# Eight single PSUM banks, sums of g by DMA and a new hand-written order in an attention and MLP kernel

## The chip, the cores and the metric

The kernel runs on one core of one Trainium2 chip. The metric is the time of the kernel on the device, in microseconds (us); of several runs the median is given. The engines that matter are TensorE (PE, matmuls), VectorE (DVE), ScalarE (ACT) and GpSimd (POOL); SP issues transfers. PE writes its results to PSUM, which has eight banks of 512 float32 columns on each of 128 partitions. DVE and ACT read them from there.

## What is computed

There are four batches of 6080 tokens with 256 channels, and q, k, v of that shape. The attention runs over channels: a 256 x 256 matrix for each batch. A token-wise MLP with 2048 hidden features follows.

```python
qn = q / (np.linalg.norm(q, axis=1, keepdims=True) + 1e-06)
kn = k / (np.linalg.norm(k, axis=1, keepdims=True) + 1e-06)
s = kn.transpose(0, 2, 1) @ qn / tau
a = softmax(s)                       # over the last axis
x = (v @ a).reshape(B * N, 256)
h = x @ w_in                         # 256 -> 2048
g = 0.5 * h * (1.0 + np.tanh(c * (h + 0.044715 * h * h * h)))
out = g @ w_out                      # 2048 -> 256
```

## The kernel before, in words

The product a @ w_in is made once for each batch ("aw", 256 x 2048 in bf16), so that the main part has two stages: h = v @ aw, then out = gelu(h) @ w_out. The tokens are cut into 25 blocks: each batch has five of 1024 tokens and one of 960, the last batch ends with 512 and 448. A block has two halves of 512 (480) tokens, and 16 chunks of 128 hidden features.

**First stage.** Chunks come in two ways. A *plain* chunk (word `g`, `plain`, L495) is two halves of two matmuls with 512 columns each. They fill a pair of PSUM banks, and one gelu over 1024 elements reads both (`G`, L511). In block 0 `e` and `E` (L522, L534) do the same for two chunks of one half. A *set* (words `m1` to `m7`, `small`, L563) makes two chunks, i and 8 + i, of both halves with seven matmuls in place of eight, by a scheme of the Strassen kind on sums of aw (`SW`) and of v (`vs`). Its additions go over ACT and DVE (`set_step`, L607): `wcq` copies bank rb into the first bank of a pair qp (ACT), `wy5` copies the second bank to SBUF (ACT), `wap` and `wax` add rb and that copy (DVE), and PE adds further products onto what they left in PSUM. `wGq` is the gelu over both banks of the pair, `wGr` and `wGx` are the gelus of the other two quarters. Over all blocks 137 pairs of chunks are sets and 110 chunks are plain.

**Second stage.** It is a scheme of the same kind with products M1 to M7 (`product`, L712), each of four matmuls for each half h of the features, on sums of g, T1 to T4 (`token_sum`, L693). They are adds of 128 x 2048 bf16 elements on DVE. In the blocks that `SUMS_DMA` (L952) names, T3 is a transfer instead: POOL issues a DMA that adds one quarter of g onto another in SBUF. M7 reads T3. `cq`, `y5`, `ap` and `ax` are the stage's additions (`mm2_step`, L765), `c11` to `c22` transpose the results on DVE (`turn`, L744), and SP stores them.

**Beside it.** For each later batch q and k are loaded in eight pieces by POOL (`lq`, `lk`). They are squared (`qsq`, `ksq`: on ACT, or on DVE where `SQ_DVE`, L949, says so), folded (`f1` to `f3`), summed on PE (`sp`) and multiplied on PE (`row`), and a chain of small steps makes that batch's aw (`aw`, `ac`). POOL casts v to bf16 in HBM (`lv`), and SP loads it transposed (`lt`).

**Order.** There is no scheduler. `ORDER` (L958) is a list of 3498 words; each word records its instructions on its engines, and every engine works through its own in that order. A word `m1.5@r:2` is product m1 of set 5 in block 2, and it takes the PSUM buffer with the tag r. There are two pairs (h, b) and four single banks (a, p, r, s). A tag is taken again only when the last reader of its earlier contents is done. POOL's loads wait for the matmul just before them in the list (`GATE`), so that they don't run ahead.

Of the kernel before, what the change touches and what calls it, by code (L numbers as in the profile page):

```python
# [16 lines left out]
def kernel(  # L17
# [228 lines left out]
    def ss_rows(c, which, rows=None):  # L246
# [3 lines left out]
        if c == 0:  # L250
            SS[which] = bank("sp"[which], [128, 2] if which == 0 else [128, 256], f"ss0{which}")
# [135 lines left out]
    def first_aw():  # L387
        b = 0
        ps0 = [bank("sp"[ic], [128, 256], f"aw_ps{ic}") for ic in range(2)]
        ps1 = bank("b", [128, 2, 512], "aw_ps")  # L390
        ps = [ps0, [ps1[:, ic, 0:256] for ic in range(2)]]
        sums = bank("a", [128, 2], "sums0")
# [92 lines left out]
    PAIR_USES = {}  # L485

    def apart(n, i, side, engine, inst):

        uses = PAIR_USES.setdefault((n, i), [])
        for other, s, e in uses:  # L490
            if s != side and e != engine:
                tc.declare_no_dep(inst.ins, other.ins.name, reason="the other bank of the pair")
        uses.append((inst, side, engine))

    def plain(n, u, tag):  # L495
# [6 lines left out]
        w = hc if wide else t
        for x in range(2):
            BITS[tag, x] = w
            for cc in range(2):
                mm(hp[:, x, :w],
                   lhsT=aw(b, cc, u if wide else 2 * u + x),
                   rhs=vt_tiles[n][:, cc, x * hc : x * hc + hc] if wide else vt_tiles[n][:, cc, :],
                   start=cc == 0, stop=cc == 1)

    def plain_gelu(n, u):  # L511
        t = BLOCKS[n][2]
        hc = t // 2
        hp = PR.pop((n, u))
        if t > 512:
            nc.scalar.activation(g_half(n, u // 8)[:, :, u % 8], hp[:, :, :hc], AF.Gelu_apprx_tanh)  # L516
        else:
            k0 = u % 4 * 2
            nc.scalar.activation(g_half(n, u // 4)[:, :, k0 : k0 + 2].rearrange("p t u x -> p u t x"),
                                 hp[:, :, :t].rearrange("p u (t x) -> p u t x", t=2), AF.Gelu_apprx_tanh)  # L520

    def half(n, p, t, tag):  # L522

        b = batch(n)
        hc = hc_of(n)
        hp = bank(tag, [128, 2, 512], f"e{n}_{p}_{t}")
        PR[n, p, t] = hp
        for x in range(2):
            BITS[tag, x] = hc
            for cc in range(2):  # L530
                mm(hp[:, x, :hc], lhsT=aw(b, cc, 2 * p + x),
                   rhs=vt_tiles[n][:, cc, t * hc : t * hc + hc], start=cc == 0, stop=cc == 1)
# [30 lines left out]
    def small(n, i, m, tag=None):  # L563
# [16 lines left out]
        if m == 1:  # L580
            RB[n, i] = bank(tag, [128, 512], f"rb{n}_{i}")
        if m == 5:
            QP[n, i] = bank(tag, [128, 2, 512], f"qp{n}_{i}")
            QTAG[n, i] = tag
            w = U * hc
            if BITS.get((tag, 0), 0) < w:
                x0 = BITS.get((tag, 0), 0) // 32 * 32
                for x in range(x0, w, 256):
                    y = min(w, x + 256)
                    mm(QP[n, i][:, 0, x:y], lhsT=ones_bf, rhs=zeros_bf[:, 0 : y - x],  # L590
                       start=x == 0, stop=True)
            BITS[tag, 0] = max(w, BITS.get((tag, 0), 0))
            BITS[tag, 1] = w
        dst = {2: 0, 3: 1, 5: 1}
        acc = QP[n, i][:, dst[m]] if m in dst else RB[n, i]
        for u in range(U):
            inst = mm(acc[:, u * hc : u * hc + hc], lhsT=lhs(u), rhs=rhs,
                      start=m in (1, 5) and u == 0, stop=u == U - 1)
            if m in dst:
                apart(n, i, dst[m], "pe", inst)  # L600
# [6 lines left out]
    def set_step(n, i, what):  # L607
# [4 lines left out]
        if what == "cq":  # L612
            apart(n, i, 0, "act", nc.scalar.activation(QP[n, i][:, 0, :w], RB[n, i][:, :w], AF.Copy))  # L613
# [11 lines left out]
        if what == "Gq":  # L625
            g = g_half(n, 0)
            qp = QP.pop((n, i))
            if U == 1:
# [136 lines left out]
    def mm2_step(n, what):  # L765
        hc = hc_of(n)
        if what == "cq":
            nc.scalar.activation(ACC[n, "p"][:, :hc], ACC[n, "r"][:, :hc], AF.Copy)
        elif what == "y5":
            XS[n] = xp.tile([128, 512], FP32, tag="y5", name=f"y5_{n}")  # L770
            nc.scalar.activation(XS[n][:, :hc], ACC[n, "p"][:, :hc], AF.Copy)
        elif what == "ap":
            nc.vector.tensor_add(ACC[n, "r"][:, :hc], ACC[n, "p"][:, :hc], XS[n][:, :hc])
# [5 lines left out]
        else:  # L779
# [9 lines left out]
    with tc.manual_schedule():
# [88 lines left out]
        def run(word):  # L878
# [42 lines left out]
            elif what == "e":  # L921
                half(n, *a, tag)
            elif what == "E":
                half_gelu(n, *a)
# [366 lines left out]
```

## Time and profile before

| | |
|---|---|
| median of 3 runs | 687.28 us (687.09 to 691.3) |
| the profiled execution | 686.68 us |
| its span, first to last instruction | 684.8 us |
| PE busy, 3584 matmuls | 666.8 us |
| ACT busy, 941 instructions | 620.5 us |
| DVE busy, 924 instructions | 614.0 us |
| POOL busy | 86.5 us |
| granted PE clock, mean | 0.998 |

A group of instructions in the profile is named by its line, engine, output and inputs; all matmuls of the main part have the line of the helper `mm`, L482, so they are told apart by tiles: h, qp and rb belong to the first stage, r and p to the second, G to the q and k products. [...] Busy time counts overlapping instructions once. A share of DMA is the time of all packets over 16 engines' time and can pass 1, as packets overlap.

### The profile page before, as it was taken

To read this page: it belongs to the slowest core of one execution; us is meant where nothing else is said; L and a number is where in the kernel's file an instruction comes from. 1 tells how busy PE (TensorE), PEld (TensorE's weight loads), DVE (VectorE), ACT (ScalarE), POOL (GpSimd) and SP (SyncE) were. 2 spreads that over 40 slices of the span, in tenths; PEclk is the share of its full clock that TensorE was granted. 3 is DMA by queue.
4 is the path that set the end of the run, shared out by engine and by line. 5 is a ranking of instruction groups with operands and counts; after the bars stand their busy time and mean duration, and the time that the engine had idled before them with its cause. 6 is when DMAs were issued, how large, how long until landed. Compare 5 with 4: busy or idle time off the path is not lost.

```text
span 684.8 us, 10307 instructions
## 1 busy us (share of the span) xinstructions
PE 666.8 (97%) x3584; PEld 336.6 (49%) x3584; DVE 614.0 (90%) x924; ACT 620.5 (91%) x941; POOL 86.5 (13%) x151
## 2 busy tenths in 40 slices
PE   3999999999999999999999999999999999999996
PEld 2854545454445454444444544545444444444566
DVE  3579999999999999979999999999999989889894
ACT  4389999998899999989989999999989999999983
POOL 4322111111001101111010010001000011101001
PEclk9999999999999999999999999999999999999999
DMA  9998989694787785875957987657274299378463
GB/s 240 208 247 144 157 152 137 106 153 78 119 119 126 134 156 87 151 114 88 166 87 126 179 136 125 94 85 122 42 113 92 35 138 162 62 119 158 90 118 64
DMA packets 163524, 86.14 MB, mean 126 GB/s; under 512 B 148736, under 2 KB 152448, under 8 KB 162752
## 3 DMA queue, kind: packets, MB, share of 16 engines
q0 software_dynamic: 16496, 47.06, 41.6%
q1 hardware_dynamic: 145728, 37.14, 31.4%
q10 hardware_dynamic: 1248, 1.28, 0.7%
q8 instruction: 28, 0.46, 0.3%
q14 instruction: 24, 0.20, 0.1%
HBM read 78.91 MB, written 36.57 MB: 169 GB/s over the span
## 4 chain that ended last, share of the span: by engine, by line
PE 91%; DMA 4%; ACT 3%; issue 1%; DVE 1%; POOL 0%; DVEq 0%; ACTq 0%; POOLq 0%
PE p L482 23%; PE r L482 18%; PE rb L482 17%; PE qp L482 12%; PE h L482 11%; PE G L205 5%; DMA qk_g1b<-in_k_dram 3%; PE e L482 2%; PE awp L374 2%; DMA qk_g1a<-in_q_dram 1%; PE o L482 1%; ACT g L639 1%; ACT g L629 1%; ACT g L516 0%; ACT qp L613 0%
## 5 line engine op out<-in xcount | busy, mean ns | idle before, releaser
L482 PEld LDWEIGHTS <-wcomb 128*128 128x128 bf16 x1408 | 136.6, 98 | 146.5 <-issue 2.8
L482 PE MATMUL p<-t,wcomb 128*128 128x512 bf16 (+2 forms) x576 | 142.2, 373 | 0.2
L482 PE MATMUL r<-g,wcomb 128*128 128x512 bf16 (+2 forms) x576 | 141.8, 373 | 0.0
L629 ACT ACTIVATE g<-qp 128x1024 bf16<-128x1024 f32 (+1 forms) x130 | 132.1, 1022 | 5.0 <-PE qp L482 4.8
L482 PEld LDWEIGHTS <-aw 128*128 128x128 bf16 x872 | 84.7, 98 | 90.7 <-DVE aw L416 1.3
L708 DVE TENSOR_TENSOR t<-g,t 128x2048 bf16<-128x2048 bf16 (+2 forms) x96 | 112.5, 1180 | 0.0
L621 DVE TENSOR_TENSOR qp<-rb,yw 128x512 f32<-128x512 f32 (+2 forms) x137 | 93.4, 686 | 14.3 <-PE rb L482 6.2
L482 PE MATMUL rb<-tv,sw 128*128 128x512 bf16 (+3 forms) x288 | 100.3, 366 | 0.4 <-ACT qp L613 0.3
L624 DVE TENSOR_TENSOR xw<-rb,yw 128x512 f32<-128x512 f32 (+2 forms) x137 | 92.1, 675 | 6.4 <-PE rb L482 3.9
L516 ACT ACTIVATE g<-h 128x1024 bf16<-128x1024 f32 (+1 forms) x92 | 94.3, 1035 | 2.1 <-PE h L482 2.1
L482 PE MATMUL h<-vT,aw 128*128 128x512 bf16 (+2 forms) x376 | 94.4, 377 | 0.0
L613 ACT ACTIVATE qp<-rb 128x512 f32<-128x512 f32 (+2 forms) x137 | 81.4, 600 | 7.8 <-PE rb L482 6.4
L619 ACT ACTIVATE yw<-qp 128x512 f32<-128x512 f32 (+2 forms) x137 | 81.8, 604 | 6.5 <-PE qp L482 5.0
L482 PEld LDWEIGHTS <-sw 128*128 128x128 bf16 x576 | 56.0, 98 | 56.3 <-issue 2.2
L639 ACT ACTIVATE g<-xw 128x512 bf16<-128x512 f32 (+1 forms) x130 | 82.6, 639 | 0.8 <-DVE xw L624 0.7
L639 ACT ACTIVATE g<-rb 128x512 bf16<-128x512 f32 (+1 forms) x130 | 77.9, 606 | 4.1 <-PE rb L482 3.7
L442 POOL DMA_DIRECT2D vb<-in_v_dram x45 | 22.9, 510 | 305.4 <-PE rb L482 137.9
L708 DVE TENSOR_TENSOR t<-g 128x2048 bf16<-128x2048 bf16 (+2 forms) x48 | 56.3, 1182 | 1.7 <-PE p L482 1.1
L482 PE MATMUL qp<-vT,sw 128*128 128x512 bf16 (+3 forms) x144 | 51.3, 366 | 0.1
L482 PE MATMUL rb<-vT,aw 128*128 128x512 bf16 (+3 forms) x144 | 51.0, 366 | 0.0
L482 PE MATMUL qp<-vT,aw 128*128 128x512 bf16 (+3 forms) x144 | 50.5, 366 | 0.0
L482 PE MATMUL rb<-tv,aw 128*128 128x512 bf16 (+3 forms) x144 | 50.3, 366 | 0.0
(144 smaller groups left out, 816.4 us busy)
## 6 DMA issues: line engine op xcount, KB each, us to landing
out_dram<-ot SPq DMA_DIRECT2D x160, 128.0 KB, 3.1
vb<-in_v_dram POOLq DMA_DIRECT2D x38, 256.0 KB, 3.9
k<-in_k_dram POOLq DMA_DIRECT2D x21, 384.0 KB, 5.9
q<-in_q_dram POOLq DMA_DIRECT2D x21, 384.0 KB, 5.3
g<-g POOLq DMA_DIRECT2D x14, 512.0 KB, 6.1
out_dram<-ot SPq DMA_DIRECT2D x24, 120.0 KB, 3.3
wst<-in_moe_w_out_dram POOLq DMA_DIRECT2D x2, 1024.0 KB, 10.4
vb<-in_v_dram POOLq DMA_DIRECT2D x6, 240.0 KB, 3.8
```

The source lines that it names most:

```text
L205: nc.tensor.matmul(G[b][:, jc, :], lhsT=qt[:np_, r, jc * 128 : jc * 128 + 128], rhs=kt[:np_, r, :], start=first and jc == 0, stop=jc == 1, ...
L374: nc.tensor.matmul(ps, lhsT=ET[b][:, jc, ic * 128 : ic * 128 + 128], rhs=win_bf[:, jc, fs * 512 : fs * 512 + 512], start=jc == 0, stop=jc ...
L442: after(nc.gpsimd.dma_start(out=vb[: y - x, :], in_=v[b, t0 + x : t0 + y, :]), gate)
L482: GATE[0] = nc.tensor.matmul(*a, skip_group_check=True, **kw)
L516: nc.scalar.activation(g_half(n, u // 8)[:, :, u % 8], hp[:, :, :hc], AF.Gelu_apprx_tanh)
L613: apart(n, i, 0, "act", nc.scalar.activation(QP[n, i][:, 0, :w], RB[n, i][:, :w], AF.Copy))
L619: apart(n, i, 1, "act", nc.scalar.activation(YW[n, i][:, :w], QP[n, i][:, 1, :w], AF.Copy))
L621: apart(n, i, 1, "dve", nc.vector.tensor_add(QP[n, i][:, 1, :w], RB[n, i][:, :w], YW[n, i][:, :w]))
L624: nc.vector.tensor_add(XW[n, i][:, :w], RB[n, i][:, :w], YW.pop((n, i))[:, :w])
L629: nc.scalar.activation(g[:, :, k0], qp[:, :, :hc], AF.Gelu_apprx_tanh)
L639: nc.scalar.activation(g[:, t, k0], x[:, :w], AF.Gelu_apprx_tanh)
L708: (nc.vector.tensor_add if add else nc.vector.tensor_sub)(o, a, b)
```

## The change

- PSUM is eight tags of one bank each (a to g, and z, which takes G, `sp`, the small results of a batch and, in the last batch, `m5`). A plain chunk is two words, one for each bank, and each has a gelu of 512 elements. `e` and `E` are gone. In a set m5 has a bank until `wy5` has copied it; the two sums that the pair held are taken when `wcq` and `wap` write them. The gelu `wGq` becomes `wGp` and `wGs`. The second stage's sums are split in the same way (r, m, p, q). `apart`, which declared the two banks of a pair independent, is gone.
- `fill` writes zeros by a matmul where a bank is wider used than a matmul has written it before. In the built order that happens eight times.
- `SUMS_DMA` names blocks 1 to 22 instead of 8, 9 and 18 to 22.
- `SQ_DVE` has 30 squares instead of 12.
- 150 sets instead of 137, so 84 plain chunks (168 half words) instead of 110.
- All 3946 words stand in a new order.

```diff
-    def gram_row(b, c, i, tag="a"):
+    def gram_row(b, c, i, tag="z"):
...
+    def fill(acc, tag, w):
+        x0 = BITS.get(tag, 0) // 32 * 32
+        for x in range(x0, w, 256):
+            mm(acc[:, x : min(w, x + 256)], lhsT=ones_bf, rhs=zeros_bf[:, 0 : min(w, x + 256) - x],
+               start=x == 0, stop=True)
+        BITS[tag] = max(w, BITS.get(tag, 0))
...
-            nc.scalar.activation(g_half(n, u // 8)[:, :, u % 8], hp[:, :, :hc], AF.Gelu_apprx_tanh)
+            nc.scalar.activation(g_half(n, u // 8)[:, x, u % 8], hp[:, :hc], AF.Gelu_apprx_tanh)
...
+    def set_sum(n, i, x, tag):
+        hc = hc_of(n)
+        Q[n, i, x] = bank(tag, [128, 512], f"q{n}_{i}_{x}")
+        fill(Q[n, i, x], tag, hc if hc > 256 else 2 * hc)
...
         if what == "cq":
-            apart(n, i, 0, "act", nc.scalar.activation(QP[n, i][:, 0, :w], RB[n, i][:, :w], AF.Copy))
+            set_sum(n, i, 0, tag)
+            nc.scalar.activation(Q[n, i, 0][:, :w], RB[n, i][:, :w], AF.Copy)
...
         if what == "ap":
-            apart(n, i, 1, "dve", nc.vector.tensor_add(QP[n, i][:, 1, :w], RB[n, i][:, :w], YW[n, i][:, :w]))
+            set_sum(n, i, 1, tag)
+            nc.vector.tensor_add(Q[n, i, 1][:, :w], RB[n, i][:, :w], YW[n, i][:, :w])
...
-        if what == "Gq":
-            g = g_half(n, 0)
-            qp = QP.pop((n, i))
-            if U == 1:
-                nc.scalar.activation(g[:, :, k0], qp[:, :, :hc], AF.Gelu_apprx_tanh)
...
-        acc = "r" if i <= 3 else "p"
+        acc = {1: "r", 2: "r", 3: "q", 4: "p", 5: "m", 6: "p", 7: "p"}[i]
...
-SUMS_DMA = {8, 9, 18, 19, 20, 21, 22}
+SUMS_DMA = {1, 2, 3, 4, 5, 6, 7, 8, 9, 10, 11, 12, 13, 14, 15, 16, 17, 18, 19, 20, 21, 22}
```

More of the change, by code (lines that the diff above doesn't have):

```diff
@@ L250, in ss_rows @@
         if c == 0:
-            SS[which] = bank("sp"[which], [128, 2] if which == 0 else [128, 256], f"ss0{which}")
+            SS[which] = bank("ab"[which], [128, 2] if which == 0 else [128, 256], f"ss0{which}")
         for r in rows:
@@ L266, in warm @@
     def warm(n):
-        w = bank("h", [128, 2, 512], "warm")
+        w = bank("c", [128, 512], "warm")
         for i in range(n):
-            nc.tensor.matmul(w[:, 0, 0:256], lhsT=ones_bf, rhs=zeros_bf, start=True, stop=True)
+            nc.tensor.matmul(w[:, 0:256], lhsT=ones_bf, rhs=zeros_bf, start=True, stop=True)
     ET, RS = {}, {}
@@ L388, in first_aw @@
         b = 0
[L389 to L392, printed above, removed]
+        ps = [[bank("abcd"[2 * f + ic], [128, 256], f"aw_ps{f}{ic}") for ic in range(2)] for f in range(2)]
+        sums = bank("z", [128, 2], "sums0")
         rs = smx.tile([128, 2], FP32, tag="rs")
@@ L483, in mm @@
         return GATE[0]
[L485 to L495, printed above, removed]
+    def fill(acc, tag, w):
[4 more added lines that the diff above has]
+        BITS[tag] = max(w, BITS.get(tag, 0))
@@ L497, in plain @@
+    def plain(n, u, x, tag):
         b, _, t = BLOCKS[n]
         hc = t // 2
-        hp = bank(tag, [128, 2, 512], f"h{n}_{u}")
-        PR[n, u] = hp
+        PR[n, u, x] = hp = bank(tag, [128, 512], f"h{n}_{u}_{x}")
         wide = t > 512
[L502 to L509, printed above, removed]
@@ L511, in plain_gelu @@
-    def plain_gelu(n, u):
+        BITS[tag] = w = hc if wide else t
+        for cc in range(2):
+            mm(hp[:, :w], lhsT=aw(b, cc, u if wide else 2 * u + x),
+               rhs=vt_tiles[n][:, cc, x * hc : x * hc + hc] if wide else vt_tiles[n][:, cc, :],
+               start=cc == 0, stop=cc == 1)
+    def plain_gelu(n, u, x):
         t = BLOCKS[n][2]
         hc = t // 2
-        hp = PR.pop((n, u))
+        hp = PR.pop((n, u, x))
         if t > 512:
-            nc.scalar.activation(g_half(n, u // 8)[:, :, u % 8], hp[:, :, :hc], AF.Gelu_apprx_tanh)
+            nc.scalar.activation(g_half(n, u // 8)[:, x, u % 8], hp[:, :hc], AF.Gelu_apprx_tanh)
@@ L517, in plain_gelu @@
         else:
[L518 to L532, printed above, removed]
@@ L581, in small @@
             RB[n, i] = bank(tag, [128, 512], f"rb{n}_{i}")
+            BITS[tag] = U * hc
         if m == 5:
[L583 to L595, printed above, removed]
-        for u in range(U):
[L597 to L600, printed above, removed]
+            M5[n, i] = bank(tag, [128, 512], f"m5{n}_{i}")
+            BITS[tag] = U * hc
+        acc = {2: lambda: Q[n, i, 0], 3: lambda: Q[n, i, 1], 5: lambda: M5[n, i]}.get(m, lambda: RB[n, i])()
+        for u in range(U):
+            mm(acc[:, u * hc : u * hc + hc], lhsT=lhs(u), rhs=rhs, start=m in (1, 5) and u == 0, stop=u == U - 1)
+    def set_sum(n, i, x, tag):
+        hc = hc_of(n)
+        Q[n, i, x] = bank(tag, [128, 512], f"q{n}_{i}_{x}")
+        fill(Q[n, i, x], tag, hc if hc > 256 else 2 * hc)
     def set_buffer(n, i, xy):
@@ L605, in set_buffer, with set_step @@
         return {"x": xp, "y": ywp}[xy].tile([128, 512], FP32, tag=f"{xy}w", name=f"{xy}w{n}_{i}")
-    def set_step(n, i, what):
+    def set_step(n, i, what, tag):
         hc = hc_of(n)
@@ L727, in product, with next_sum @@
                start=first and kk == 0, stop=kk == 3)
+    def next_sum(n, acc, tag):
+        hc = hc_of(n)
+        ACC[n, acc] = bank(tag, [128, 512], f"{acc}{n}")
+        fill(ACC[n, acc], tag, hc)
     def direct(n, p, t, tag):
@@ L763, in store, with mm2_step @@
                 in_=ot[bi * 32 : bi * 32 + 32, 0 : hc // 32].rearrange("p x h c -> p x (h c)"))
[L765 removed]
+    def mm2_step(n, what, tag):
         hc = hc_of(n)
         if what == "cq":
+            next_sum(n, "p", tag)
             nc.scalar.activation(ACC[n, "p"][:, :hc], ACC[n, "r"][:, :hc], AF.Copy)
@@ L785, in mm2_step @@
             else:
-                src = ACC[n, {"c11": "r", "c12": "r", "c21": "p"}[what]]
+                src = ACC[n, {"c11": "r", "c12": "q", "c21": "p"}[what]]
             turn(n, ci, tj, src)
@@ L927, in run @@
             elif what[0] == "w":
-                set_step(n, *a, what[1:])
+                set_step(n, *a, what[1:], tag)
             elif what[0] == "T":
@@ L937, in run @@
             else:
-                mm2_step(n, what)
+                mm2_step(n, what, tag)
         for word in ORDER.split():
@@ new lines @@
+sa.1:1 ax:0 ksq.2:1 f1.2:1 M4.1:0 m5.6@e:1 wax.5:1 c12:0 lk.4:1 f2.2:1 M4.0:0 g.11_1@b:1 f3.2:1
+sp.2@z:1 c21:0 wGs.5:1 G.12_1:1 sa.2:1 wGx.5:1 wy5.6:1 g.7_0@a:1 g.15_0@g:1 g.15_1@e:1 wap.6@c:1
+ksq.3:1 row.2_1@z:1 m3.6:1 row.3_1:1 m4.5:1 qsq.3:1 G.15_1:1 wGs.6:1 G.11_1:1 f1.3:1 row.3_0:1
+m7.6:1 row.3_3:1 G.7_0:1 row.3_5:1 row.2_0:1 wax.6:1 g.0_0@e:2 lk.5:1 T1.0:1 g.12_0@c:2 lq.5:1
+T3.0:1 f2.3:1 row.3_4:1 wGr.5:1 m4.6:1 m1.3@b:2 G.0_0:2 m1.1@a:2 g.4_0@d:2 row.2_5:1 row.2_2:1
+row.2_3:1 vs:2 G.12_0:2 wcq.3@e:2 m5.1@c:2 G.15_0:1 wGr.6:1 m6.3:2 m2.3:2 T1.1:1 wcq.1@g:2 wy5.1:2
@@ new lines @@
+T4.1:2 wap.6@b:3 lk.0:2 wcq.7@e:3 m3.6:3 m5.7@g:3 f3.7:1 m7.6:3 sp.7@z:1 T1.0:3 m6.7:3 wGx.5:3
+wax.6:3 wy5.7:3 sa.7:1 wGx.6:3 m2.7:3 wap.7@g:3 M3.1:2 M4.1:2 wGs.6:3 wGp.7:3 c12:2 lq.0:2 m7.7:3
+m4.6:3 wax.7:3 m3.7:3 g.0_1@b:4 wGr.6:3 wGs.7:3 m4.7:3 c21:2 vs:4 m1.1@d:4 m1.2@e:4 G.0_1:4 T1.1:3
+wcq.1@c:4 row.7_5@z:1 row.6_5:1 wGr.7:3 m5.1@g:4 row.7_4:1 lv.1:5 m2.1:4 row.7_0:1 m5.2@a:4
+row.6_1:1 m6.1:4 pow:1 row.6_0:1 wcq.2@b:4 wy5.1:4 wGx.7:3 m2.2:4 wy5.2:4 wap.1@f:4 kf:1 T3.1:3
+T3.0:3 wGp.1:4 wGp.2:4 m6.2:4 row.7_2:1 row.7_3:1 m7.1:4 m1.3@g:4 wcq.3@a:4 wax.1:4 row.7_1:1
@@ new lines @@
+sa.1:2 ksq.2:2 T3.1:6 lq.5:2 wap.2@d:7 M1.1@e:6 M1.0:6 m3.2:7 m7.2:7 wax.1:7 wGp.2:7 y5:6 m4.1:7
+f1.2:2 lv.0:9 m5.5@c:7 m6.3:7 cq@f:6 f2.2:2 wy5.5:7 f3.2:2 wGr.1:7 wGx.1:7 M2.0:6 m5.3@c:7 M6.1:6
+sp.2@z:2 g.4_1@a:7 wGs.2:7 wax.2:7 m1.5@d:7 m4.2:7 M6.0:6 wy5.3:7 G.4_1:7 c22:5 wGr.2:7 wGx.2:7
+wcq.5@c:7 M2.1:6 wap.3@a:7 ap@b:6 m3.3:7 sa.2:2 lv.1:9 ksq.3:2 wGs.3:7 m7.3:7 m6.5:7 M3.0:6
+row.2_3@z:2 qsq.3:2 m2.5:7 row.2_4:2 wap.5@a:7 row.3_1:2 m3.5:7 c11:6 wGp.5:7 lq.6:2 wax.3:7 m7.5:7
+row.3_4:2 g.0_1@e:7 m5.7@c:7 m4.3:7 wGs.5:7 T4.0:6 m1.6@a:7 row.2_1:2 wGx.3:7 G.0_1:7 M3.1:6
@@ new lines @@
+row.2_5:2 wcq.6@e:7 f1.3:2 f2.3:2 wax.5:7 T4.1:6 m2.6:7 M7.0:6 c12:6 lk.4:2 m6.6:7 wGr.3:7 m1.7@g:7
+wGp.6:7 M7.1:6 m4.5:7 wy5.7:7 wcq.7@e:7 m5.6@c:7 m6.7:7 ax:6 row.2_0:2 m2.7:7 lk.5:2 M4.0:6 wy5.6:7
+wap.7@b:7 wap.6@c:7 m3.7:7 row.3_2:2 wGr.5:7 g.12_1@d:7 m7.6:7 wGp.7:7 T1.0:7 m3.6:7 wGx.5:7 wGs.7:7
+row.3_3:2 row.2_2:2 g.0_0@e:8 wGs.6:7 wax.6:7 m4.6:7 m7.7:7 row.3_5:2 m1.1@b:8 row.3_0:2 wGx.6:7
+wax.7:7 G.0_0:8 g.12_0@c:7 T3.0:7 wGr.6:7 m4.7:7 G.12_1:7 g.8_1@e:8 gc:2 f3.3:2 G.12_0:7 wcq.1@a:8
@@ new lines @@
+row.4_2:2 M4.0:7 wcq.1@g:9 row.4_1:2 m4.6:8 row.4_4:2 c21:7 m4.7:8 G.8_0:9 f2.5:2 wGs.7:8 T3.0:8
+g.4_0@f:8 m1.2@b:9 vs:9 wGx.7:8 m2.1:9 wGr.7:8 g.0_0@a:9 row.5_2:2 G.4_0:8 T1.1:8 f3.5:2 wcq.2@d:9
+row.4_3:2 m5.1@f:9 G.0_0:9 wy5.1:9 row.5_0:2 row.4_5:2 m2.2:9 row.4_0:2 g.12_0@a:8 m6.1:9 g.8_1@f:9
+gc:2 m6.2:9 wGp.1:9 wGp.2:9 g.0_1@g:9 wap.1@d:9 T2.1:8 wGr.6:8 G.12_0:8 m5.3@e:9 sp.5@z:2 m5.2@a:9
+m7.1:9 T3.1:8 lv.0:11 G.8_1:9 wy5.2:9 qsq.6:2 wax.1:9 wy5.3:9 G.0_1:9 lq.0:3 sa.5:2 T2.0:8 M1.1@f:8
@@ new lines @@
+m4.1:12 M2.1:11 wGp.5:12 wGr.1:12 wax.2:12 m5.5@g:12 ksq.1:3 T2.0:11 m4.2:12 m6.5:12 m1.6@e:12
+wGs.2:12 M2.0:11 wy5.5:12 wGr.2:12 wap.5@f:12 c11:11 M6.1:11 c22:10 m5.6@g:12 row.1_0:3 m3.5:12
+m5.7@b:12 M6.0:11 qsq.1:3 lk.3:3 wcq.6@d:12 wGs.5:12 wy5.6:12 T4.0:11 wGx.2:12 m2.6:12 m6.6:12
+m7.5:12 ap@f:11 wGp.6:12 g.8_1@g:12 M3.1:11 wax.5:12 M3.0:11 wy5.7:12 wGx.5:12 wap.6@d:12 m7.6:12
+lq.3:3 G.8_1:12 m4.5:12 g.12_0@b:12 m1.7@g:12 T4.1:11 c12:11 f1.1:3 wax.6:12 m3.6:12 M7.0:11
+wcq.7@f:12 wGr.5:12 wGs.6:12 m6.7:12 m2.7:12 G.12_0:12 wGx.6:12 g.12_1@a:12 M7.1:11 wap.7@d:12
@@ new lines @@
+wy5.7:13 wGr.3:13 wcq.6@a:13 m2.6:13 m6.6:13 wy5.6:13 wGx.5:13 wGr.5:13 row.3_0:3 qsq.3:3 lv.0:16
+row.2_4:3 row.2_3:3 T4.1:12 m1.7@g:13 g.12_1@f:13 M7.0:12 wcq.7@c:13 G.12_1:13 T4.0:12 c12:12
+wap.6@e:13 m7.6:13 m6.7:13 f1.3:3 wax.6:13 wap.7@f:13 lq.5:3 m3.6:13 M7.1:12 wGx.6:13 ax:12 f2.3:3
+m4.6:13 m2.7:13 row.2_1:3 wGp.6:13 m7.7:13 row.2_0:3 M4.1:12 wGs.6:13 lk.5:3 wGr.6:13 wax.7:13
+f3.3:3 T1.0:13 m3.7:13 m4.7:13 m1.1@a:14 row.3_5:3 g.4_1@e:13 M4.0:12 vs:14 T3.0:13 m5.1@d:14
+wGx.7:13 wGr.7:13 wcq.1@g:14 wGp.7:13 row.2_5:3 row.3_1:3 m6.1:14 G.4_1:13 m2.1:14 m1.2@c:14
@@ new lines @@
+wy5.1:14 wGs.7:13 wcq.2@e:14 row.2_2:3 c21:12 wap.1@d:14 g.8_1@b:14 m5.2@f:14 m7.1:14 m2.2:14
+row.3_2:3 G.8_1:14 m3.1:14 T1.1:13 wy5.2:14 T3.1:13 wGp.1:14 m6.2:14 g.8_0@b:14 gc:3 wax.1:14
+wGp.2:14 M5.0@f:13 sp.3@z:3 M5.1:13 m1.5@g:14 wap.2@e:14 wGs.1:14 wGx.1:14 G.8_0:14 ksq.4:3
+g.12_0@d:13 m4.1:14 T2.0:13 qsq.4:3 y5:13 wcq.5@b:14 lq.6:3 lk.6:3 wGr.1:14 m7.2:14 m3.2:14
+g.0_1@f:14 wGs.2:14 G.12_0:13 m6.5:14 m2.5:14 m5.5@a:14 M1.0@e:13 wax.2:14 wy5.5:14 f1.4:3 M1.1:13
+wap.5@d:14 G.0_1:14 wGx.2:14 wGp.5:14 m4.2:14 g.0_0@a:14 cq@f:13 T2.1:13 m3.5:14 m7.5:14 m5.3@b:14
```

633 lines of the change are left out of this document (314 added, 319 removed).

## The prediction

> **What bounds the kernel now.** I read the busy shares first, then the chain of work that ended last, then the busy time by stretches, then who waits for whom on PE, and last the timelines of ACT, DVE and the DMA queues. The page says PE is busy for 97% of the span and is 91% of the chain:
>
> ```profile
> PE 666.8 (97%) x3584; PEld 336.6 (49%) x3584; DVE 614.0 (90%) x924; ACT 620.5 (91%) x941; POOL 86.5 (13%) x151
> ...
> PE 91%; DMA 4%; ACT 3%; issue 1%; DVE 1%; POOL 0%; DVEq 0%; ACTq 0%; POOLq 0%
> ```
>
> In the stretches the columns are length, busy time of PE, weight loads, DVE, ACT and POOL, the granted clock, DMA share and GB/s:
>
> ```profile
> 0.00:40.00 40.00, 27.79 (x258) 21.10 (x259) 18.92 (x39) 18.97 (x24) 16.88 (x31) 1.00 1.08 221
> 40.00:200.00 160.00, 159.67 (x832) 77.58 (x830) 152.94 (x230) 152.09 (x219) 21.57 (x40) 1.00 0.82 139
> 200.00:360.00 160.00, 159.85 (x822) 77.36 (x820) 148.91 (x224) 150.67 (x229) 19.40 (x33) 1.00 0.74 124
> 360.00:520.00 160.00, 160.00 (x827) 77.89 (x826) 153.83 (x230) 152.19 (x232) 14.41 (x27) 1.00 0.67 109
> 520.00:680.00 160.00, 159.47 (x853) 82.69 (x851) 139.05 (x203) 146.62 (x242) 14.25 (x20) 1.00 0.65 108
> 680.00:685.00 5.00, 0.00 (x0) 0.00 (x0) 0.40 (x2) 0.00 (x0) 0.00 (x0) 0.68 0.53 93
> ```
>
> From 40 to 680 us PE is idle for 640 - 638.99 = 1.0 us. ACT is idle there for 38.4 us (busy 601.6), DVE for 45.3 (busy 594.7). So PE's own work sets the time, and the other two run some 6% below it. The only wait of PE after 40 us that the view of waits lists is one of 0.3 us:
>
> ```profile
> PE rb L482 <- ACT qp L613: 0.3, 1, 0.3
> ```
>
> There is nearly nothing to gain from waits, and much to lose: every wait that the change creates on PE is paid in full.
>
> **The change on PE.** A set of seven products replaces two plain chunks of four matmuls each. 13 more sets are 91 matmuls more and 26 plain chunks are 104 less: 13 fewer. A matmul of 512 columns costs a quarter of such a piece of the chain (start, length, what):
>
> ```profile
> 651.84 0.86 PE p L482 x4
> ```
>
> so 0.215 us, and 13 x 0.215 = -2.8 us. Counted in the built order, eight small fills come in (seven of 32 columns, one of 192), 416 columns in all. By columns that is 0.2 us; the nearest rows bound it by 0 and by 8 x 0.14 = 1.1 (warm, 256 columns: 5.4 us for 38). I take 0.2. PE's sum: -2.6 us.
>
> **ACT.** Every gelu of two banks becomes two of one bank. The cost of an instruction in a full queue is the distance from its start to the next one's (start, duration, ...):
>
> ```profile
> 412.57 0.59 ACT L639 ACTIVATE g<-rb 128x512 bf16<-128x512 f32 x1
> 413.05 1.03 ACT L516 ACTIVATE g<-h 128x1024 bf16<-128x1024 f32 x1
> 413.95 0.62 ACT L639 ACTIVATE g<-rb 128x512 bf16<-128x512 f32 x1
> 414.43 1.06 ACT L516 ACTIVATE g<-h 128x1024 bf16<-128x1024 f32 x1
> 415.33 0.65 ACT L613 ACTIVATE qp<-rb 128x512 f32<-128x512 f32 x1
> 415.85 0.65 ACT L639 ACTIVATE g<-xw 128x512 bf16<-128x512 f32 x1
> ```
>
> Wide 0.90, narrow from PSUM 0.48: two narrow ones are 0.96, or 0.06 more. 137 sets and the 84 plain chunks that are left make 221 x 0.06 = +13.3 us. A new set costs 0.52 + 0.48 + 3 x 0.48 + 0.52 = 2.96 (copy, y5, three gelus from PSUM, one from SBUF) against 2 x 0.90 = 1.80 for two plain chunks: 13 x 1.16 = +15.1. 18 squares go to DVE: 15 of 1536 elements at 1.37 (rows at 402.61 and 403.98) and 3 shorter ones with their rest rows at about 1.5: -25.0. Sum: +3.4 us, which the 38.4 us of idle time cover.
>
> [...]
>
> **DVE.** 15 more blocks give the third sum of g to DMA: 30 adds of 2048 elements at 1.13 (rows at 409.85 and 410.98) are -33.9. 26 more adds of the new sets at 0.60 (410.98 to 411.58) are +15.6. The 18 squares cost 15 x 0.87 (416.03 to 416.90) + 3 x 0.9 = +15.8. Sum: -2.5 us, and nothing on the path; 45.3 us of idle time cover it either way.
>
> **Accumulating DMAs.** 14 become 44, 512 KB each, on POOL and its queue q0. What is known of them: the page's lines, the landings of the view by line, and SP's transposes beside the two slowest (issued at 548.6 and 553.4):
>
> ```profile
> q0 software_dynamic: 16496, 47.06, 41.6%
> ...
> g<-g POOLq DMA_DIRECT2D x14, 512.0 KB, 6.1
> ```
>
> ```profile
> DMA to landing us min/median/max: 4.5/6.1/10.6
> ```
>
> ```profile
> 547.13 2.75 SPq L447 DMA_TRANSPOSE vT<-vb x2
> ```
>
> POOL issues 30 more at 0.88 us, 26 us on an engine that is 13% busy. The four products of M7 wait for the landing, and behind them stands all of PE; M4, the output sums, transposes and stores of the block follow. The cover is the matmul time that the new order puts between the words T3 and M7. The shortest: block 16 7.8 us (17 small matmuls, 4 products of four, 2 aw parts), block 7 8.3, block 2 8.9, blocks 5, 9, 18 and 21 9.1, block 17 9.8, block 22 10.2; the longest 22.7. In the profile the least time left between landing and M7 was 0.9 us, at a landing of 9.3 (block 18). So a usual landing of 6.1 is covered everywhere; one of 10.6 at each of those nine places costs 2.8 + 2.3 + 1.7 + 4 x 1.5 + 0.8 + 0.4 = 14.0 us. A gain is excluded: PE did not wait for the adds on DVE. The bounds are 0 and 14.0. I take 0.5, near the lower end, because 12 of the 14 landed within 9 us.
>
> DMA load grows. q0's share is 285 us for 47.06 MB, 3.2 us of all 16 engines for one such transfer, 30 of them 95 us or 14 points on a mean of 74%. From 40 to 200 us, with next-batch loads of q and k, 0.82 becomes about 1.05. The stretch of 20 us from 400 ran at a share of 1.00, and its loads landed in 3.8 to 7.0 us. The new order places q and k loads at least 8.2 us of matmuls ahead of their squares, as before, and the latest v load (block 3, second half) 14.5 us ahead of its first matmul, against 3.9 for the cast and 4.2 for the transpose. On POOL a waiting sum holds back the loads behind it; on SP the transposes still wait for stores ahead of them, and have 8.5 us or more. I cost this at nothing; if that cover goes, it falls under the second rival.
>
> **Banks.** Pairs held from m5 to Gq go away. The new order takes a bank that another engine must first release 932 times instead of 502, the middle distance in matmul time being 0.9 us in both. No row shows what a hand-over more costs; the old 502 cost PE at most the 1.0 us of idle time, 0.002 each; at 0.03 each, a tenth of the one wait listed, 430 more would be 13. I take +0.8, twice the idle time for twice the hand-overs, with bounds of -1.0 (all idle time gone) and +13. All steps have moved; sums over stretches of 20 us of matmuls give ACT at most 22.5 and DVE at most 21.1, before 21.5 and 21.3, so neither gets a stage of its own.
>
> **Sum.** Span 684.8 - 2.6 + 0.5 + 0.8 = 683.5. The profiled execution took 686.68, 1.9 more than its span, and the median 687.28 is 0.6 above that: 686.0 us.
>
> **The rivals.**
> 1. Forecast: PE stays the bound, little moves: 686.0, by its bounds 683.7 (no wait left) to 690. Chance 0.73.
> 2. The sums land late, which ends on the other side: landings near 10.6 us in the loaded blocks, PE stands at M7 nine times: 687.28 - 2.6 + 14.0 = 698.7. For it: the two that were issued within 6.3 us of that pair of transposes took 10.6 and 9.3, and every block has transposes. Against it: one at 571.5, beside a transpose too, landed in 6.2, and the other eleven in 7.8 or less. It decides from 9.7 us of waits, about 0.2 us for each of 44. Chance 0.13.
> 3. ACT becomes the bound. If a split costs the difference of durations, 2 x 0.60 - 1.02 = 0.18, it is 39.8 us and ACT's sum +29.9. Of its 38.4 us of idle time 19.9 wait for PE (6.4, 5.0, 4.8 and 3.7 in the view of waits), so it decides from 18.5 more: 11.4 too many, 687.28 - 2.6 + 11.4 = 696. Against it: the starts above. Chance 0.05.
> 4. Hand-overs of banks stall PE, 13 us: 697.7. Chance 0.05.
> 5. Faster by over 1%, below 680.4: the 2.6, the 1.0 of idle time and some 3.5 more from the first 40 us, where PE is idle for 12.2 us, mostly for loads that the change leaves alone. Chance 0.04.
>
> **How the numbers follow.** The likeliest is the first, 686.0, its own range 683 to 690. The range for 8 in 10 reaches to the second, third and fourth: 681.5 to 698.7. A difference under 1% is about what a measurement of this kernel can't tell from no change. Faster by over 1% 0.04, within 1% 0.73, slower 0.23.
>
> **What would show it.** PE busy near 664, PE's idle time from 40 to 680 us under 4 us, ACT busy for about 624 us and DVE for 612, 44 sums landing in 5 to 9 us, no wait of PE on M7. I am wrong if PE waits for DMA or ACT for more than 7 us in all, or if landings lie above 10 us.

## The result and the profile after

The changed kernel takes 690.34 us (median of 20 runs, 690.0 to 695.73), the kernel before 687.12 (20 runs). The ratio is 1.0048, 95% interval 1.0036 to 1.0061: slower by half a per cent. 686.0, slightly faster, had been forecast. The profiled execution took 690.15 us with a span of 688.0, 3.2 more than before.

The first lines of the page after, busy time and shares of the chain, answer to the first fence of the prediction:

```profile
PE 662.0 (96%) x3517; PEld 336.1 (49%) x3579; DVE 612.6 (89%) x941; ACT 621.9 (90%) x1193; POOL 115.0 (17%) x181
...
PE 87%; ACT 7%; DVE 2%; DMA 2%; issue 1%; SPq 0%; DVEq 0%; ACTq 0%
```

PE works less than before (662.0 for 666.8), and yet the span is longer: PE's share of the chain fell from 91% to 87%, ACT's rose from 3% to 7%. PE now waits for something. Of 3579 weight loads only 3517 have their matmul in this trace; the 62 missing records lower PE's busy time, so it overstates how much PE lost. The stretches (length, busy time of PE, weight loads, DVE, ACT, POOL, granted clock, DMA share, GB/s):

```profile
0.00:40.00 40.00, 27.66 (x258) 21.26 (x260) 18.79 (x38) 19.48 (x25) 16.73 (x31) 1.00 1.07 221
40.00:200.00 160.00, 158.49 (x822) 77.78 (x837) 153.93 (x240) 150.21 (x287) 29.16 (x47) 1.00 0.94 166
200.00:360.00 160.00, 157.41 (x796) 76.28 (x810) 150.77 (x232) 151.53 (x295) 27.35 (x42) 1.00 0.90 150
360.00:520.00 160.00, 157.76 (x796) 76.59 (x811) 149.19 (x229) 151.46 (x294) 25.11 (x38) 1.00 0.85 145
520.00:680.00 160.00, 157.83 (x824) 81.60 (x837) 138.48 (x201) 148.16 (x294) 16.66 (x23) 1.00 0.64 115
```

The first 40 us are as before, the clock is full (1.00 in each stretch), ACT and DVE are no busier. The DMA share rose by 0.12 to 0.18 in the stretches from 40 to 520 us, and fell by 0.01 in the last. What PE waits for is in the view of waits (engine, tile, line, the releaser with its tile and line; us in all, times, longest):

```profile
PE q L481 <- DVE q L745: 1.6, 3, 0.8
...
PE q L481 <- ACT q L584: 1.2, 2, 0.7
PE h L481 <- DVE aw L415: 1.1, 1, 1.1
PE rb L481 <- DVE q L593: 0.8, 1, 0.8
PE r L481 <- ACT p L739: 0.7, 1, 0.7
PE h L481 <- DVE aw L386: 0.3, 1, 0.3
PE h L481 <- ACT yw L590: 0.2, 1, 0.2
PE m L481 <- ACT yw L590: 0.2, 1, 0.2
```

Before, one wait of 0.3 us was all there was after 40 us. The two on `aw` belong to the start of the main part, and the first was there before (0.8 us, from 38 us on). The seven on L745, L584, L593 and L739 have one thing in common: these lines write the copy or the add that opens a sum, `cq`, `ap`, `wcq` or `wap`. One of the places, in a timeline (start, duration, engine, line, what; in brackets the idle time before, and what ended it):

```profile
343.22 0.37 PE L481 MATMUL q<-vT,sw 128*128 128x480 bf16 x1
...
343.42 0.18 PE L481 MATMUL p<-zeros_bf,ones_bf 128*128 128x32 bf16 x1
...
343.66 0.58 ACT L739 ACTIVATE p<-r 128x512 f32<-128x512 f32 x1 [1.17 <-PE p L481]
...
344.29 1.02 PE L481 MATMUL r<-g,wcomb 128*128 128x512 bf16 x4 [0.69 <-ACT p L739]
```

The second line is one of the eight fills. Word `cq` records it together with its copy, so it stands in PE's queue behind all that was recorded earlier. The bank was free by then: in the first experiment below the same copy starts about 1 us earlier, beside the same matmuls. ACT's copy writes over the same bank and must follow the fill: ACT stands idle for 1.17 us until PE has come to it. Then PE itself stands for 0.69 us, because its next products M2 add onto r only after the copy has read r. Neither engine was short of time; each waited for the other once.

From the starts I sum what every distance from one matmul to the next has over its usual length (0.216 us for 512 columns, 0.202 for 480, and so on); where a record is missing, its usual length is taken off as well. From 40 us to the end that excess is 6.2 us before and 12.0 after. Over the whole span, the matmuls' usual lengths sum to 656.1 and 653.6. So the change is -2.5 + 5.8 = +3.3 us, against +3.2 in the span. Only differences between kernels are read from this excess: with the median distance of each shape as its usual length, the level is some 2 us lower in all of them. At the eight fills the distances are too long by this much:

| fill at | who writes the sum | PE work between its word and the first product that needs it, us | excess, us |
|---|---|---|---|
| `cq` block 10 | ACT | 0 | 0.84 |
| `wcq` set 6, block 12 | ACT | 0 | 0.84 |
| `wcq` set 2, block 18 | ACT | 0.22 | 0.62 |
| `cq` block 4 | ACT | 1.07 | none |
| `ap` block 10 | DVE | 0 | 0.96 |
| `wap` set 1, block 24 | DVE | 0 | 0.95 |
| `ap` block 4 | DVE | 0.42 | 0.54 |
| `ap` block 16 | DVE | 0.43 | 0.53 |

So a fill at the copy costs 0.84 us less the PE work behind it, one at the add 0.96 less that work, and the eight 5.3 us together. The two waits on `yw` (L590), 0.35 us of distance each, come 1 us behind two fills at `wcq`: ACT, late with that copy, is late with this one, a gelu later, too. With them it is 6.0 us. That is the theory that the runs test: *late fills*. Its rivals: the DMA load of the 30 new sums (vb landed in 5.5 us for 3.9 before), or the splitting of gelus and the hand-overs of single banks. All ratios below are to the kernel before, on the same chip, with their 95% interval.

### The profile page after: what moved, and what is told of

It reads as the page before. It is cut to its first block, busy times and chain, and to the rows that moved or that the text cites. A ratio compares the mean times of both kernels' runs of the same rounds, so it can differ in the third digit from the quotient of the medians.

```text
span 688.0 us, 10545 instructions
## 1 busy us (share of the span) xinstructions
PE 662.0 (96%) x3517; PEld 336.1 (49%) x3579; DVE 612.6 (89%) x941; ACT 621.9 (90%) x1193; POOL 115.0 (17%) x181
## 4 chain that ended last, share of the span: by engine, by line
PE 87%; ACT 7%; DVE 2%; DMA 2%; issue 1%; SPq 0%; DVEq 0%; ACTq 0%
PE rb L481 17%; PE p L481 16%; PE q L481 13%; PE r L481 11%; PE m L481 10%; PE h L481 10%; PE G L205 6%; ACT g L602 3%; PE awp L375 2%; DMA qk_f<-in_q_dram 1%; ACT q L584 1%; PE o L481 1%; ACT yw L590 1%; PE warm L269 1%; PE ss L263 1%
## 5 line engine op out<-in xcount | busy, mean ns | idle before, releaser
L602 ACT ACTIVATE g<-q 128x512 bf16<-128x512 f32 (+1 forms) x286 | 170.8, 621 | 5.3 <-PE q L481 4.4
L593 DVE TENSOR_TENSOR q<-rb,yw 128x512 f32<-128x512 f32 (+2 forms) x150 | 102.1, 686 | 13.6 <-PE rb L481 4.1
L510 ACT ACTIVATE g<-h 128x512 bf16<-128x512 f32 (+1 forms) x164 | 97.1, 654 | 4.1 <-PE h L481 4.0
L584 ACT ACTIVATE q<-rb 128x512 f32<-128x512 f32 (+2 forms) x150 | 91.4, 618 | 8.1 <-PE q L481 3.3
L590 ACT ACTIVATE yw<-m 128x512 f32<-128x512 f32 (+2 forms) x150 | 92.7, 621 | 6.2 <-PE m L481 3.7
L481 PE MATMUL r<-g,wcomb 128*128 128x512 bf16 (+2 forms) x377 | 94.2, 373 | 1.2 <-ACT p L739 0.7
L481 PE MATMUL p<-t,wcomb 128*128 128x512 bf16 (+2 forms) x372 | 93.3, 373 | 0.5
L665 POOL DMA_DIRECT2D g<-g x44 | 39.5, 933 | 180.3 <-ACT g L602 78.2
L481 PE MATMUL m<-tv,sw 128*128 128x512 bf16 (+3 forms) x156 | 56.1, 367 | 0.4 <-ACT yw L590 0.2
L481 PE MATMUL q<-vT,aw 128*128 128x512 bf16 (+3 forms) x153 | 54.1, 367 | 1.2 <-ACT q L584 1.2
```

Source lines behind the costliest of these rows:

```text
L481: GATE[0] = nc.tensor.matmul(*a, skip_group_check=True, **kw)
L510: nc.scalar.activation(g_half(n, u // 8)[:, x, u % 8], hp[:, :hc], AF.Gelu_apprx_tanh)
L584: nc.scalar.activation(Q[n, i, 0][:, :w], RB[n, i][:, :w], AF.Copy)
L590: nc.scalar.activation(YW[n, i][:, :w], M5.pop((n, i))[:, :w], AF.Copy)
L593: nc.vector.tensor_add(Q[n, i, 1][:, :w], RB[n, i][:, :w], YW[n, i][:, :w])
L602: nc.scalar.activation(g[:, t, k0], x[:, :w], AF.Gelu_apprx_tanh)
```

## The experiments

**Fills put where the bank is free.** The changed kernel, but each fill is recorded right behind the matmul that took the same bank before; it widens what that matmul wrote, long before the copy.

```diff
+    def widen(what, n, acc, tag, w):
+        if (what, n) in WIDEN:
+            x0, x1 = BITS[tag] // 32 * 32, WIDEN[what, n]
+            mm(acc[:, x0:x1], lhsT=ones_bf, rhs=zeros_bf[:, 0 : x1 - x0], start=False, stop=True)
+            BITS[tag] = x1
...
+WIDEN = {("g.0_0", 5): 512, ("m5.2", 5): 512, ("m5.4", 11): 512, ("m5.7", 11): 512, ("M1.1", 11): 512,
+         ("m5.6", 17): 512, ("m1.7", 17): 512, ("M1.0", 23): 448}
```

> The changed kernel with its eight fills at another place: each directly behind the matmul that took the same bank before, when PE still owns it, and none at the copies and adds. Theory (late fills): seven of the eight fills make ACT or DVE wait until PE gets there, and then PE waits for their copy or add; the waits seen are 0.84 (four times about, with 0.62 where 0.22 us of matmuls lie between), 0.54, 0.96, 0.84, 0.53, 0.62 and 0.95, 5.3 us in all. Without them 690.3 - 5.3 = 685.0 us. Rival (load of the accumulating DMAs) and rival (more hand-overs of banks): fills cost 0.2 us, 690 us stays.

Measured: 683.85 us, ratio 0.9962 (0.9948 to 0.9976). This kernel is faster than both. Of its waits of PE in the main part only these two are listed:

```profile
PE h L481 <- DVE aw L415: 1.1, 1, 1.1
...
PE h L481 <- DVE aw L386: 0.3, 1, 0.3
```

The same place as above, in its timeline:

```profile
342.13 0.58 ACT L750 ACTIVATE p<-r 128x512 f32<-128x512 f32 x1 [0.15 <-PE r L481]
...
342.71 0.37 PE L481 MATMUL q<-vT,sw 128*128 128x480 bf16 x1
...
342.91 1.03 PE L481 MATMUL r<-g,wcomb 128*128 128x512 bf16 x4
```

ACT now waits 0.15 us, and for r, which it needs; the copy is done while PE works, and M2 starts 0.20 us behind its forerunner, without idle time. The same eight fills, the same columns: only their place differs, and it is worth 6.5 us in the medians (690.34 to 683.85) and 6.1 in the spans of the profiled executions (688.0 to 681.9), about what the eight direct waits and the two behind them add up to. The excess falls to 5.9 us, the level of before. What is left of the change is 2.9 us of span less than before, 2.5 of them by the fewer matmuls.

**Late fills alone, in the kernel before.** Eight copies of sets in the old order get a fill that they don't need, of the full width: two matmuls of 256 columns.

```diff
+            if (n, i) in LATE:
+                for x in (0, 256):
+                    apart(n, i, 0, "pe", mm(QP[n, i][:, 0, x : x + 256], lhsT=ones_bf, rhs=zeros_bf,
+                                            start=x == 0, stop=True))
...
+LATE = {(4, 1), (4, 4), (6, 1), (6, 6), (9, 1), (10, 6), (12, 2), (15, 3)}
```

> The kernel before with one part of the change alone: at the copy of rb in eight sets PE first writes zeros over the bank (two matmuls of 256 columns, 0.22 us), in the order just where the copy stands; behind it comes m6 or m2 of the same set with nothing between. Theory (late fills): each costs its 0.22 plus the 0.84 us of PE waiting for the copy, 8 x 1.06 = 8.5, so 687.1 + 8.5 = 695.6 us, less where ACT was late anyway. Rivals: only the matmuls' own 1.7 us, 688.9 us.

Measured: 699.17 us, ratio 1.018 (1.0166 to 1.0193). The direction and the place are right, the size is a miss: +12.4 for 8.5. The waits of PE:

```profile
PE rb L482 <- ACT qp L617: 5.3, 8, 0.7
...
PE qp L482 <- ACT qp L617: 0.7, 1, 0.7
PE rb L482 <- DVE qp L625: 0.6, 1, 0.6
PE qp L482 <- DVE qp L625: 0.5, 1, 0.5
```

The eight on L617 follow the fills, 0.7 us each (0.89 of distance too much in the starts). That is 7.1 us. The fills' own columns are 16 x 0.11 = 1.8 us. The rest, some 3 us, lies in follow-on waits like the last two lines: the stall that ACT and DVE suffered is paid again, later. I had counted only the stall itself.

**Without the new sums.** The changed kernel with its late fills, but the transfers of blocks 1 to 7 and 10 to 17 are not issued; M7 reads a quarter of g without that sum.

```diff
+        if i == 3 and n in LEFT_OUT:
+            return
...
+LEFT_OUT = {1, 2, 3, 4, 5, 6, 7, 10, 11, 12, 13, 14, 15, 16, 17}
```

> The changed kernel without the third sum of g in blocks 1 to 7 and 10 to 17 (left out: neither DMA nor add, M7 reads the quarter as it is). Theory (late fills): no wait of PE on M7 is listed, so nothing falls, 690.3 us within 0.7. Rival (load): 95 us of the 16 engines' time fall away, the landings get back to 6 us, and the excess over the kernel before goes: 687 us or less.

Measured: 690.26 us, ratio 1.0047 (1.0035 to 1.0059): no different from the changed kernel's 1.0048. The DMA share is down by 0.14 to 0.22 in the stretches from 40 to 520 us, and the casts of v land in 3.9 us again, but PE's busy time in each is the same to 0.01 us:

```profile
40.00:200.00 160.00, 158.48 (x822) 77.80 (x837) 153.91 (x239) 150.22 (x287) 21.93 (x39) 1.00 0.80 140
200.00:360.00 160.00, 157.41 (x795) 76.27 (x809) 150.78 (x232) 151.58 (x295) 19.99 (x34) 1.00 0.76 125
360.00:520.00 160.00, 157.76 (x797) 76.65 (x811) 149.14 (x229) 151.50 (x295) 14.02 (x26) 1.00 0.63 105
```

The casts of v in this run, with the same line as before the change (KB each, median us to landing):

```profile
vb<-in_v_dram POOLq DMA_DIRECT2D x38, 256.0 KB, 3.9
```

And in the changed kernel:

```profile
vb<-in_v_dram POOLq DMA_DIRECT2D x38, 256.0 KB, 5.5
```

So the accumulating transfers do slow other loads (these casts from 3.9 to 5.5 us), and cost nothing here (690.34 us with the 30, 690.26 without). The load as a cause has fallen.

**Split gelus alone, in the kernel before.** Every gelu of two banks becomes two of one bank; the order, the pairs and all else stay.

```diff
-            nc.scalar.activation(g_half(n, u // 8)[:, :, u % 8], hp[:, :, :hc], AF.Gelu_apprx_tanh)
+            for x in range(2):
+                nc.scalar.activation(g_half(n, u // 8)[:, x, u % 8], hp[:, x, :hc], AF.Gelu_apprx_tanh)
...
-                nc.scalar.activation(g[:, :, k0], qp[:, :, :hc], AF.Gelu_apprx_tanh)
+                for x in range(2):
+                    nc.scalar.activation(g[:, x, k0], qp[:, x, :hc], AF.Gelu_apprx_tanh)
```

> The kernel before with every gelu over two banks (130 of sets, 92 of plain chunks) as two of one bank each, nothing else. By the distance of starts, 0.06 us for each split: ACT busy 620.5 + 13 = 634 us, and the time within 1.5 us of 687.1, as ACT has 38 us of idle time. By the difference of durations, 0.18 for each: ACT +40 us, the time near 696. [...]

Measured: 693.63 us, ratio 1.0097 (1.0084 to 1.011). Half of the expectation was right. ACT's line on the page:

```profile
PE 668.9 (97%) x3522; PEld 336.5 (49%) x3584; DVE 615.7 (89%) x924; ACT 632.6 (91%) x1163; POOL 86.8 (13%) x151
```

632.6 - 620.5 = 12.1 us for 222 more instructions, 0.055 each: the distance from start to start, 0.06, had been the right price, and not the difference of durations, 0.18. But the time rose by 6.9 us where ACT's idle time was to cover it: the excess on PE went from 6.2 to 13.2 us, in many waits of 0.1 to 0.5 us. The view of waits lists only the longest of them:

```profile
PE rb L482 <- ACT qp L614: 0.7, 2, 0.4
PE rb L482 <- DVE qp L622: 0.3, 1, 0.3
PE qp L482 <- ACT g L517: 0.3, 1, 0.3
PE p L482 <- DVE t L710: 0.2, 1, 0.2
```

In the kernel before, ACT was busy for 91% and hardly made PE wait (0.3 us listed); breaking the gelus up made the waits. This was a surprise, and the next three runs follow it.

**Squares back on ACT.** The first experiment's kernel, the fastest, with the 12 squares on DVE of before in place of 30.

```diff
-SQ_DVE = {('k', 1, 0), ('k', 1, 1), ('k', 1, 2), ('k', 1, 3), ('k', 1, 4), ('k', 1, 5), ('k', 1, 6), ('k', 1, 7), ('k', 2, 0), ...
+SQ_DVE = {('k', 1, 0), ('k', 1, 2), ('k', 1, 4), ('k', 1, 6), ('k', 2, 0), ('k', 2, 2), ('k', 2, 4), ('k', 2, 6), ('k', 3, 0), ...
```

> The changed kernel with early fills, and 18 of the squares back on ACT. ACT's busy time should be 622.2 + 25.0 = 647, DVE's 612.9 - 15.8 = 597. If idle time in sum covers added work (ACT is idle for about 60 of 682 us), the time stays at 684 to 685. If, as the split gelus alone showed (ACT +12.1 us, time +6.9), an order written for one load passes about 0.57 of each added us on to PE, it is 683.85 + 0.57 x 25 = 698. Waits of PE on ACT in the stretches up to 520 us, where the squares lie, and none after, speak for the second.

Measured: 706.09 us, ratio 1.0284 (1.0267 to 1.0301). ACT's busy time is 646.5, as expected (+24.3), and the time rises by 22.2 us: nine tenths of it, more than the 0.57 I had carried over from the split gelus. The excess is 27.8 us from 40 to 520 us, where the squares lie, and 0.3 after. The first of them, in ACT's part of the timeline and then in PE's:

```profile
51.64 3.17 ACT L517 ACTIVATE g<-h 128x512 bf16<-128x512 f32 x6
54.50 1.66 ACT L158 ACTIVATE sq<-q 128x1536 bf16<-128x1536 bf16 x1
55.88 1.76 ACT L517 ACTIVATE g<-h 128x512 bf16<-128x512 f32 x3
```

```profile
54.52 1.03 PE L481 MATMUL h<-vT,aw 128*128 128x512 bf16 x4
56.70 0.59 PE L481 MATMUL h<-vT,aw 128*128 128x512 bf16 x2 [1.16 <-ACT g L517]
```

One square holds ACT for 1.38 us between gelus; the gelu behind it frees its bank late, and PE stands for 1.16 us.

**Sums back on DVE.** The first experiment's kernel with the transfers of before.

```diff
-SUMS_DMA = {1, 2, 3, 4, 5, 6, 7, 8, 9, 10, 11, 12, 13, 14, 15, 16, 17, 18, 19, 20, 21, 22}
+SUMS_DMA = {8, 9, 18, 19, 20, 21, 22}
```

> The changed kernel with early fills, and the third sum of g in blocks 1 to 7 and 10 to 17 back on DVE: 30 adds at 1.13 us, DVE's busy time 612.9 + 33.9 = 647. If DVE's idle time of some 69 us covers them, the time stays at 684 to 685, and the accumulating transfers pay nothing by themselves. If the rate of the split gelus (0.57 us of PE for each added us) holds for DVE as well, it is 683.85 + 19.3 = 703, with waits of PE on DVE in blocks 1 to 7 and 10 to 17 (about 40 to 200 and 270 to 490 us) and none in the rest.

Measured: 714.94 us, ratio 1.0415 (1.0399 to 1.0431). DVE's busy time rises by 645.1 - 612.9 = 32.2 us, the time by 31.1. The waits of PE, and one of them in the timeline:

```profile
PE rb L481 <- DVE xw L605: 6.4, 8, 1.9
PE q L481 <- DVE q L602: 5.7, 7, 1.8
PE rb L481 <- DVE q L602: 3.9, 5, 1.7
```

```profile
149.10 2.35 DVE L680 TENSOR_TENSOR g<-g,g 128x2048 bf16<-128x2048 bf16 x2
...
151.37 0.68 DVE L605 TENSOR_TENSOR xw<-rb,yw 128x512 f32<-128x512 f32 x1
...
152.11 0.38 PE L481 MATMUL rb<-tv,aw 128*128 128x512 bf16 x1 [1.85 <-DVE xw L605]
```

The two adds stand in DVE's queue ahead of `wax` (L605). Bank rb stays taken until that add has read it, and PE's next product into it waits 1.85 us. The long waits lie where the returned adds are; behind the last of them, from 562 us on, there are none. At the rate of the split gelus 703 was expected; nearly all of the added time came through, not 0.57 of it. Giving these sums to DMA is worth 31 us in this order.

**Split gelus, with the squares moved.** The kernel of the fourth experiment with the 30 squares on DVE of the changed kernel.

```diff
-SQ_DVE = {('k', 1, 0), ('k', 1, 2), ('k', 1, 4), ('k', 1, 6), ('k', 2, 0), ('k', 2, 2), ('k', 2, 4), ('k', 2, 6), ('k', 3, 0), ...
+SQ_DVE = {('k', 1, 0), ('k', 1, 1), ('k', 1, 2), ('k', 1, 3), ('k', 1, 4), ('k', 1, 5), ('k', 1, 6), ('k', 1, 7), ('k', 2, 0), ...
```

> The kernel before with every two-bank gelu as two one-bank gelus, and 18 squares moved from ACT to DVE as in the changed kernel: ACT 632.6 - 25 = 608, DVE 614 + 15.8 = 630. Split gelus alone took 693.63. If the 6.9 us came from ACT's added busy time, which is now given back twice over, the time returns to 686 to 688. If they came from the split itself (the second bank of a pair, and with it the next start into that pair, comes 0.06 us or more later each time, in an order that leaves no slack), it stays at 691 to 694. If DVE's 15.8 us pass on at 0.57, it is 695 or more, with waits of PE on DVE near the squares.

Measured: 701.04 us, ratio 1.0207 (1.0192 to 1.0223), 7.4 more than without the move, though ACT's busy time fell by 20.2 us (632.6 to 612.4). DVE's rose by 14.0, and the long waits after 60 us are for DVE now, but for one of 0.4 us on ACT:

```profile
PE rb L482 <- DVE xw L625: 1.7, 3, 0.7
PE qp L482 <- DVE qp L622: 1.4, 2, 0.8
...
PE rb L482 <- DVE qp L622: 1.1, 3, 0.6
```

The third theory fits: what DVE gets is paid on PE, at 7.4 / 14.0 = 0.53. What the run leaves open is how much of the split's 6.9 us was ACT's load and how much the later release of the second bank: the two were not separated, since the load taken from ACT came down on DVE. The traces lean to the release. Sorted by the engine that ended them, the distances that are too long make about 2 us on ACT before, 6 to 7 with the gelus split, and still 5.5 here, though ACT is now less busy than before the split (612.4 for 620.5 us); on DVE they make 2, 4 and 12 us. It is no proof, as waits on DVE shift ACT's work too.

The excess of PE accounts for the spans of all these kernels:

| kernel | excess from 40 us, us | span, us |
|---|---|---|
| before | 6.2 | 684.8 |
| changed | 12.0 | 688.0 |
| fills early | 5.9 | 681.9 |
| late fills in before | 15.9 | 696.4 |
| split gelus in before | 13.2 | 691.8 |
| squares back on ACT (fills early) | 28.1 | 704.0 |
| sums back on DVE (fills early) | 37.1 | 713.2 |
| split gelus, squares moved, in before | 20.6 | 699.0 |

## Why the prediction was wrong, point by point

- **The step that failed** is the fills in PE's sum: "By columns that is 0.2 us; the nearest rows bound it by 0 and by 8 x 0.14 = 1.1", and "I take 0.2." Measured, they cost 5.3 us directly and 6.1 to 6.5 with what follows from them. They were priced as PE work, by columns, and both bounds were of that kind. A fill is also a *hand-over*: PE, then ACT or DVE, then PE again. The prediction said that every wait that the change creates on PE is paid in full, but looked for none here. The built order would have shown it: seven of the eight had less than 0.5 us of PE work between the fill and the first product that needs its sum. The kernel before can write such zeros too, but at `m5`, where PE itself takes the pair, and its trace has none after 40 us: the change moved the fill to the copy and the add.
- **PE's products**: forecast -2.8 + 0.2, measured -2.5 in usual lengths. Right. The two terms put on top, 0.5 and 0.8, are seen in no run; without them the sum is 687.28 - 2.6 = 684.7 us, and the early-fill kernel, at 0.9962 of 687.28, takes 684.7 (683.7 to 685.6 by the interval). So the rest of the sum was sound, and the miss lies in the fills.
- **ACT and DVE**: forecast sums of about 624 and 612, measured 621.9 and 612.6. Right. "Which the 38.4 us of idle time cover" came out true for a weaker reason than was given. Four runs put 12 to 32 us on an engine that was idle for longer than that, and 53 to 97% of it came through to the time. It is the new order, written for this load, that left no waits in the early-fill kernel, not the idle sum.
- **Accumulating transfers**: forecast 0.5, with 44 landings in 5 to 9 us. PE never waited at M7, and taking 30 of them out changed nothing. Right, and the second rival is out. Four landed above 9 us, none above the mark of 10:

```profile
DMA to landing us min/median/max: 4.5/6.6/9.8
```

- **DMA load**: costed at nothing, and it cost nothing (690.26 us without the new sums, 690.34 with them), though the casts of v landed in 5.5 us for 3.9. The share from 40 to 200 us rose to 0.94, less than the 1.05 of the estimate.
- **Hand-overs of banks**: forecast +0.8. With the fills early, the excess is 5.9 us for 6.2 before: they cost nothing that can be seen. The fourth rival is out. The price itself had a weak base: "at most the 1.0 us of idle time" counts only what PE's busy time leaves open, and a matmul of 512 columns is busy for 0.38 us where the next can start after 0.216. By the starts, PE lost 4 to 6 us before the change.
- **ACT as the bound**: the third rival took 0.18 us for each split and an ACT sum of +29.9. Measured, a split cost 0.055 in the kernel before, and ACT's busy time rose by 1.4 with the change (621.9 for 620.5). It is out.
- The mark "PE waits for DMA or ACT for more than 7 us in all" was not reached after the start; the waits were on ACT *and* DVE, at most 0.8 us each, and spread over the span. The mark of 4 us of idle time from 40 to 680 us was passed: it is 640 - 631.49 = 8.5 us. Some 3 of them are gaps that the missing records leave; the early-fill kernel, with as many missing, has 4.0 up to its last matmul. The time lay inside the wide range and just outside the likeliest one's own (683 to 690).

## What to carry to other kernels

An instruction that only prepares a buffer belongs where the buffer becomes free, not where it is next used: recorded late, the fill in the timeline, 0.18 us long, made ACT wait 1.17 us for PE's queue, and PE 0.69 us in turn, and moving the eight was worth 6.5 us (690.34 to 683.85). Its own length mattered little: with no work behind it, a fill of 32 columns at a copy cost 0.84 us of distance, one of 512 columns 0.89 and its own 0.22. Price a small added instruction by the round trip that it opens, less the work that stands between its ends, and look that work up in the built order. Idle time in sum was no cover in these orders written by hand, where 53 to 97% of the work added in four runs came through to the time: ask, place by place, what is queued behind the added work and which bank it holds.

## What the runs showed of the hardware

- A matmul of 32 columns, 0.18 us long, that a copy on ACT must follow before PE goes on, opens a round trip of 0.84 us (0.96 by an add on DVE) for 512 columns, less the PE work queued in between.
- A gelu of two banks split in two costs ACT 0.055 us more of busy time; in an order without slack, that 12.1 us became 6.9 us of the kernel's time.
- 30 accumulating transfers (24 of 512 KB, six of 480) add 0.14 to 0.22 to the DMA share over 480 us and make casts of 256 KB land in 5.5 us for 3.9, and the time of this kernel, bound by PE, does not change.
